# Keys' features through VectorE and DRAM, and sums over both value halves at once, in an attention and Fourier kernel

## The chip, the core and the metric

The kernel runs on one core of a Trainium2 chip. The time is in device microseconds (us) for one execution; the profile is one further execution, recorded by the hardware profiler. The core's engines are TensorE (PE in the profile; PEld are its weight loads), VectorE (DVE), ScalarE (ACT), GpSimd (POOL) and SyncE (SP), which in this kernel issues all DMAs. Each engine works off its instructions in the order in which the program has them, and waits at an instruction until its operands are ready.

## The reference

Two independent parts, written side by side into the output. The first is an attention with a memory over four segments of 512 tokens, with 32 heads of 18 features; the second is a Fourier mixing made of matrix products.

```python
q, k, v = (x @ w, split into H=32 heads of Dh=18, N=4 segments of L=512 for w in (wq, wk, wv))
phi = lambda t: jnp.where(t > 0, t + 1.0, jnp.exp(t))
g = _sigmoid(beta)
M, z = 0, 0
for s in range(N):
    qs, ks, vs = q[:, :, s], k[:, :, s], v[:, :, s]
    logits = jnp.einsum("bhqd,bhkd->bhqk", qs, ks) * scale + mask      # causal within the segment
    a_dot = jnp.einsum("bhqk,bhkd->bhqd", _softmax(logits), vs)
    pq = phi(qs)
    num = jnp.einsum("bhld,bhde->bhle", pq, M)
    den = jnp.einsum("bhld,bhd->bhl", pq, z)[..., None] + 1e-6
    outs.append(g * (num / den) + (1.0 - g) * a_dot)
    pk = phi(ks)
    M = M + jnp.einsum("bhld,bhle->bhde", pk, vs)
    z = z + jnp.einsum("bhld->bhd", pk)
a = concat(outs) @ wo
b = dft_seq_re @ (x2 @ dft_hid_re.T) - dft_seq_im @ (x2 @ dft_hid_im.T)
return jnp.concatenate([a, b], axis=-1)
```

The memory M (18x18 a head) and its normaliser z sum over all keys of the segments before. The change is about phi of the keys, the sums M and z, and the lookup num / den.

## The kernel before, in words

All products that need more than bf16 run in two or three passes: an operand is split into a high part (`hi`, rounded to fp32r) and a low part (the rest), and hi*hi, hi*lo and lo*hi are added.

The first stage projects one segment after the other, s = 0 to 3. Its order is written out by hand; every engine gets its instructions in the order of the Python code, and `later(n, ...)` puts a piece of work `n` ticks further down (there is a tick behind each projection and behind each block of values). For a segment:

- Nine projection tiles of 128 features x 512 tokens, m = 0 to 8, each a chain of 14 matmuls. Tiles 0 to 3 are queries, 4 to 7 are keys, and tile 8 holds the last 64 features of both. `open_qk` interleaves the first four; `project_qk` runs the others and evacuates all nine. The order in segments 1 to 3 is 0, 1, 2, 3, 8, 4, 5, 6, 7, and in segment 0 it is 0 to 8.
- Evacuation of a tile: ScalarE copies it to bf16 (`p`), VectorE subtracts (`r`), and later ScalarE or POOL and POOL again cut `r` into two more bf16 parts. The three go to DRAM (`qd`, `kd`) for the second stage. `p` has four buffers and `r` three.
- In segments 1 to 3 the queries also pass through phi: a Relu and an Exp on ScalarE, `scalar_tensor_tensor` on VectorE, a rounding copy to `pq_hi` on VectorE and the difference to `pq_lo` on POOL. In PSUM two engines never read one tile at a time; the program makes each wait for the other.
- In segments 0 to 2 ScalarE copies the key tiles to `kf` in fp32. They lie with features on partitions, and the sums need tokens on partitions.
- Four blocks of 128 tokens, j = 0 to 3: `project_v` (two chains of 14 matmuls over 288 columns) and its evacuation, with the two halves of `lookup` behind the two chains (segments 1 to 3). Then `k_natural` turns the block's keys with five TensorE transposes into the PSUM tile `kt`, and runs phi on the result (`kn` hi and lo). One block late, `accumulate` adds phi(k) times v into `m_ps`: three passes over five groups of 128 features, each with the eight heads that the group touches. The last block's sums run inside the next segment's `open_qk`.
- `memory` copies `m_ps` out, zeroes what lies off the heads' diagonal (POOL) and splits the result into `md_hi` and `md_lo`. `lookup` multiplies `pq` by it: three passes over five groups of 152 columns.

PSUM has eight banks: here `kt` takes two, `m_ps` two, and projections, values and lookups share four (`acc`).

The second stage, behind 235 us, is the attention within the segments, interleaved with the Fourier products; then follow the rest of these and the output product. The diff does not touch them.

Of the kernel before, what the change touches and what calls it, by code (L numbers as in the profile page):

```python
# [23 lines left out]
P = 128  # L24
# [4 lines left out]
HEAD0 = [0, 7, 14, 21, 24]  # L29
NPAIR = 108  # L30
# [8 lines left out]
def infini_attention_and_fnet(ctx: ExitStack, tc: tile.TileContext, xT, wqk, w8, wv, wo, beta, xtT, cT, hT, out):  # L39
# [10 lines left out]
    vd = [dram.tile([P, 4, 8, 220], BF16, name=f"vd{s}") for s in range(NSEG)]  # L50
    amd = [dram.tile([4, P, D], F32, name=f"amd{s}") for s in range(NSEG)]
# [15 lines left out]
    ident = const.tile([P, P], F32, name="ident")  # L67
    identity(ident)
# [74 lines left out]
    WQ = weight(wide_tile(L))  # L143
# [4 lines left out]
    for k in range(5):  # L148
        load_x(0, k)
        raw = load_w(wqk[:, :, :L], L, k)  # L150
        split_x(0, k)
        split_wk(WQ, k, raw)
    dma(g, bass.AP(tensor=beta.tensor, offset=beta.offset, ap=[[0, P], [1, H]]))
    WK, WV = weight(wide_tile(L)), weight(wide_tile(D))
    for k in range(5):
        if k < 2:
            raw = sb.tile([P, L], F32, name="r", tag="r", bufs=3)
            dma(raw, wqk[k, :, L:])
        else:
            raw = load_w(wqk[:, :, L:], L, k)  # L160
        later((1, 1, 1, 1, 2)[k], split_wk, WK, k, raw)
# [18 lines left out]

    pq_hi = sb.tile([P, 5, L], F32R, name="pq_hi")
    pq_lo = sb.tile([P, 5, L], F32R, name="pq_lo")
    zeros_r(pq_hi[64:, 4, :])
    zeros_r(pq_lo[64:, 4, :])
# [3 lines left out]
    for i in range(2):  # L188
        kn.append(tuple(sk.tile([P, D], F32R, name=f"kn{n}{i}") for n in "hl"))
        a, b = (sk.tile([P, H, 19], F32R, name=f"vn{n}{i}") for n in "hl")  # L190
        pool.memset(a.bitcast(F32)[:, :, DH:], 1.0)
        zeros_r(b[:, :, DH:])
        vn.append((a, b))
# [4 lines left out]
    md_hi, md_lo = (sb.tile([P, 5, 8, 19], F32R, name=f"md{n}") for n in "hl")  # L198
    m_ps = [ps.tile([P, 3, 8, 19], F32, name=f"m{b}", bufs=1) for b in range(2)]

    def phi(pool_, name, src, n, hi, lo):
        e = pool_.tile([P, src.shape[-1]], F32, name=f"{name}e", bufs=2)[:n]
# [3 lines left out]
        dve.tensor_copy(hi, e)  # L206
        pool.tensor_tensor(lo, e, hi.bitcast(F32), OP.subtract)
# [10 lines left out]
    FIRST, KF = {}, {}  # L218

    def warm_up():  # L220
        o = ps.tile([P, 1024], F32, name="kt", bufs=1)
# [3 lines left out]
    def open_qk(s):  # L225
        for m in range(4):
            FIRST[m] = ps.tile([P, L], F32, name="qk", tag="acc", bufs=4)
        terms = [qk_terms(s, m) for m in range(4)]
        edges = (0, 6, 14) if s else (0, 3, 6, 9, 14)
        for a, b in zip(edges, edges[1:]):  # L230
            for m in range(4):
                for n in range(a, b):
                    pe.matmul(FIRST[m], *terms[m][n], start=n == 0, stop=n == 13)  # L233
                if s and m == 0 and a:
                    accumulate(3, (2,))
# [768 lines left out]
```

## Time and profile before

| | us |
|---|---|
| median of 3 runs | 1009.86 |
| lowest, highest | 1009.55, 1011.33 |
| the profiled execution's own time | 1009.58 |
| its span in the profile | 1007.8 |

The page of the profile gives each engine's busy time and share of the span with its number of instructions, a line of the span in 40 slices, the DMA queues, and the chain of work that ended last. A group row names line, engine, operation, output <- inputs, shapes and count, then busy us and mean ns of one, then the engine's idle time ahead of it and who ended it. A timeline row is start in us, duration in us, engine, line, operation; in square brackets stands the idle time before it and its releaser. A row by windows is the stretch, its length, busy us of PE, PEld, DVE, ACT and POOL (instructions in brackets), the granted clock, the DMA share and GB/s. In a row of one line or tile the three durations are least, median and most in ns. Matmuls are pipelined, so that one's recorded duration is longer than its place in the stream; the places are read from the starts.

### The profile page before, as it was taken

How to read it: one execution, taken by the hardware profiler on the slowest of the kernel's cores; microseconds unless marked ns; L12 is line 12 of the kernel's file. 1: busy time of each engine (PE TensorE's matmuls, PEld its weight loads, DVE VectorE, ACT ScalarE, POOL GpSimd, SP SyncE). 2: the span in 40 equal slices, each digit the busy share in tenths (PEclk: the TensorE clock that was granted, in tenths of full speed). 3: DMA queues.
4: the chain of work that ended last, by engine and by line, in shares of the span. 5: the costliest groups of instructions: out<-in, count | busy, mean ns of one | idle time of the engine just before them, and what ended most of it. 6: DMA issues, size and time to landing. Idle time of an engine off the chain costs nothing.

```text
span 1007.8 us, 25664 instructions
## 1 busy us (share of the span) xinstructions
PE 997.1 (99%) x9384; PEld 931.9 (92%) x9384; DVE 735.1 (73%) x1995; ACT 710.8 (71%) x1654; POOL 641.8 (64%) x701
## 2 busy tenths in 40 slices
PE   9999999999999999999999999999999999999998
PEld 8988989899899999999999999999989999999998
DVE  6645647575678777788898778888888889998321
ACT  7656567554777778787878788886767778777243
POOL 2657585776666776766776777767767666768100
PEclk9999999999999999999999999999999999999999
DMA  7538456687467998899999998788999999987565
GB/s 254 179 101 256 183 165 236 206 277 239 128 168 198 224 220 218 195 223 241 222 260 219 239 206 185 175 211 226 226 211 235 232 245 224 257 197 183 132 160 136
DMA packets 305038, 208.92 MB, mean 207 GB/s; under 512 B 206224, under 2 KB 259600, under 8 KB 304912
## 3 DMA queue, kind: packets, MB, share of 16 engines
q1 hardware_dynamic: 304912, 207.29, 80.3%
q8 instruction: 73, 1.20, 0.5%
q14 instruction: 53, 0.43, 0.1%
HBM read 121.32 MB, written 57.93 MB: 178 GB/s over the span
## 4 chain that ended last, share of the span: by engine, by line
PE 83%; DVE 5%; ACT 5%; issue 2%; DMA 2%; POOL 2%; SPq 1%; POOLq 0%; DVEq 0%; ACTq 0%
PE d L518 38%; PE s L678 7%; PE d L80 6%; PE v L80 4%; PE pv L796 4%; PE qk L233 4%; PE d L563 3%; PE d L564 3%; PE d L565 3%; PE pv L797 2%; PE m L326 2%; PE qk L80 2%; PE look L351 1%; PE t L752 1%; PE t L755 1%
## 5 line engine op out<-in xcount | busy, mean ns | idle before, releaser
L684 DVE CUSTOM_DVE_ANT_0 s<-s,causal 128x128 f32<-128x128 f32 (+3 forms) x512 | 250.1, 499 | 80.4 <-PE s L678 73.1
L518 PE MATMUL d<-wide,chi 128*128 128x288 f32 x1408 | 266.3, 306 | 0.8 <-DVE y L587 0.8
L405 POOL TENSOR_TENSOR clo<-craw,chi 128x512 fp32r<-128x512 f32 x158 | 215.0, 1361 | 66.6 <-ACT chi L400 47.0
L518 PEld LDWEIGHTS d<-wide,chi 128*128 128x128 f32 x1408 | 211.8, 189 | 2.7 <-DVE y L587 1.0
L518 PE MATMUL d<-wide,clo 128*128 128x288 f32 x704 | 177.5, 319 | 0.0
L718 POOL TENSOR_TENSOR hl<-pf,hl 128x768 f16<-128x768 f32 x64 | 113.9, 1779 | 42.5 <-ACT hl L714 30.3
L678 PE MATMUL s<-ks,qs 108*128 108x128 bf16 (+3 forms) x512 | 134.0, 304 | 2.7 <-DVE negm L684 2.4
L764 ACT ACTIVATE phi<-t 128x384 f16<-128x384 f32 x128 | 61.7, 482 | 105.8 <-PE t L761 105.7
L707 ACT ACTIVATE pf<-s,nb 128x128 f32<-128x128 f32 (+3 forms) x256 | 128.3, 527 | 6.2
L518 PE MATMUL d<-ab,chi 128*128 128x288 f32 x640 | 126.0, 306 | 0.0
L518 PEld LDWEIGHTS d<-wide,clo 128*128 128x128 f32 x704 | 118.6, 189 | 1.7
L779 DVE TENSOR_TENSOR plo<-pf,phi 128x384 f16<-128x384 f32 (+1 forms) x128 | 115.8, 905 | 0.0
L400 ACT ACTIVATE chi<-craw 128x512 fp32r<-128x512 f32 x160 | 100.1, 626 | 6.5 <-DMA craw<-xtT 4.2
L765 ACT ACTIVATE pf<-t 128x384 f32<-128x384 f32 (+1 forms) x192 | 99.5, 518 | 5.2 <-PE t L752 5.0
L518 PEld LDWEIGHTS d<-ab,chi 128*128 128x128 f32 x640 | 98.5, 189 | 0.6
L714 ACT ACTIVATE hl<-pf 128x768 f16<-128x768 f32 (+1 forms) x128 | 87.4, 730 | 2.0
L518 PE MATMUL d<-ab,clo 128*128 128x288 f32 x320 | 84.8, 314 | 0.0
L563 PE MATMUL d<-wide,chi 128*128 128x288 f32 x256 | 84.0, 328 | 0.0
L564 PE MATMUL d<-wide,chi 128*128 128x288 f32 x256 | 75.6, 295 | 0.0
L565 PE MATMUL d<-wide,clo 128*128 128x288 f32 x256 | 75.5, 295 | 0.0
L718 DVE TENSOR_TENSOR hl<-pf,hl 128x512 f16<-128x512 f32 x64 | 70.3, 1098 | 0.0
L779 POOL TENSOR_TENSOR plo<-pf,phi 128x384 f16<-128x384 f32 x64 | 59.9, 936 | 9.3 <-ACT pf L765 8.2
(198 smaller groups left out, 2526.7 us busy)
## 6 DMA issues: line engine op xcount, KB each, us to landing
craw<-cT SPq DMA_DIRECT2D x128, 256.0 KB
ks<-kd SPq DMA_DIRECT2D x32, 432.0 KB
qs<-qd SPq DMA_DIRECT2D x32, 432.0 KB
craw<-xtT SPq DMA_DIRECT2D x32, 320.0 KB
vd<-vs SPq DMA_DIRECT2D x16, 440.0 KB
vst<-vd SPq DMA_DIRECT2D x32, 220.0 KB
qd<-p SPq DMA_DIRECT2D x16, 384.0 KB
kd<-p SPq DMA_DIRECT2D x16, 384.0 KB
```

Of the source, the lines that this page charges most:

```text
L80: pe.matmul(o, a, b, start=n == 0, stop=n == len(terms) - 1)
L400: act.activation(hi, raw[:, :4], AF.Copy)
L405: engine.tensor_tensor(lo, raw[:, :4], hi.bitcast(F32), OP.subtract)
L518: pe.matmul(o[h], a, b[:, h * 288:h * 288 + 288], start=start, stop=stop)
L563: pe.matmul(o, xh[:, k], wl[k][:, cs], start=k == 0, stop=False)
L564: pe.matmul(o, xh[:, k], wh[k][:, cs], start=False, stop=False)
L565: pe.matmul(o, xl[:, k], wh[k][:, cs], start=False, stop=False)
L678: pe.matmul(o[:, c:c + w], q[:, i * P:w], k[:, :w], start=True, stop=True)
L684: dve.tensor_tensor_reduce(o[:, c:c + w], o[:, c:c + w], CAUSAL[0][:, L - w:], scale=scale, scalar=-LOWEST, op0=OP.add, op1=OP.min, accum_ ...
L707: act.activation(f[:, FIRST_COL[i]:FIRST_COL[i] + w], o[:, c:c + w], AF.Exp, bias=nb[:, i:i + 1], scale=-1.0)
L718: engine.tensor_tensor(hl[:, 1, a:b], f[:, a:b], hl[:, 0, a:b], OP.subtract)
L779: (pool if kind == 2 else dve).tensor_tensor(lo[:, a:b], f[:, a:b], hi[:, a:b], OP.subtract)
```

## The change

- The order of the tiles is turned round: keys first (4, 5, 6, 7, 0, 1, 8, 2, 3 in segment 0; 8, 4, 5, 6, 7, 0, 1, 2, 3 in segments 1 and 2; segment 3 keeps its order). The keys' weights are loaded and split ahead of the queries'.
- phi of the keys is computed in `project_qk`, on the projected tile, as that of the queries is. VectorE transposes the result in blocks of 32x32 (`key_features`), and four DMAs a tile (two for tile 8) write the blocks to a scratch in DRAM, `kx`, in token order, in pieces of 32 features (128 bytes). Each block of 128 tokens is read back whole (`key_load`) and split into hi and lo (`key_split`). The TensorE transposes, `kf`'s copies and `kt` go.
- `accumulate` works on six groups of heads (`KEYED`), six heads or two each. The value halves hi and lo lie side by side in one tile, so that one matmul with the high keys takes both; a second takes the low keys with the high values: two passes over six groups for three over five.
- `memory` adds the two halves, zeroes off-diagonal parts, and moves the pieces by 12 small DMAs into `mg`, in the five groups of 128 features that the lookup uses. `md` holds both halves side by side.
- `lookup` takes both halves in one pass for three of the five groups; for the fifth, the low part of the queries stands in the unused partitions 64 to 127 of `pq_hi`. 11 matmuls for 15.
- PSUM: `kt` goes, `m_ps` takes three banks for two, `acc` five for four.

```diff
+KEYED = ((0, 6, 0, 0), (6, 6, 0, 6), (12, 6, 1, 0), (18, 6, 1, 6), (24, 6, 2, 0), (30, 2, 2, 6))
...
+    kx = [dram.tile([L, D], F32, name=f"kx{s}") for s in range(NSEG - 1)]
...
+    def feature_map(pool_, name, src):
+        e = pool_.tile([P, L], F32, name=f"{name}e", bufs=2)[:src.shape[0]]
         act.activation(e, src, AF.Relu, scale=-1.0)
         act.activation(e, e, AF.Exp, scale=-1.0)
         dve.scalar_tensor_tensor(e, src, 0.0, e, op0=OP.max, op1=OP.add)
-        dve.tensor_copy(hi, e)
-        pool.tensor_tensor(lo, e, hi.bitcast(F32), OP.subtract)
+        return e
+    def query_features(m, e):
+        if m < 4:
+            dve.tensor_copy(pq_hi[:, m], e)
+            pool.tensor_tensor(pq_lo[:, m], e, pq_hi[:, m].bitcast(F32), OP.subtract)
+        else:
+            dve.tensor_copy(pq_hi[:64, 4], e)
+            pool.tensor_tensor(pq_hi[64:, 4], e, pq_hi[:64, 4].bitcast(F32), OP.subtract)
+    def key_features(s, m, e):
+        t = sk.tile([P, 16, 32], F32, name="kt", tag="kf", bufs=5)
+        dve.transpose(t.rearrange("p b j -> p (b j)"), e)
+        for a in range(4) if m < 8 else (2, 3):
+            f = (m - 4) * P + 32 * a if m < 8 else L + 32 * (a - 2)
+            later(2, dma, kx[s].rearrange("(b i) f -> i b f", i=32)[:, :, f:f + 32], t[32 * a:32 * a + 32])
+    def key_load(s, j):
+        KR[j] = sk.tile([P, D], F32, name="kr", tag="kf", bufs=5)
+        dma(KR[j], kx[s][j * P:(j + 1) * P])
+    def key_split(j):
+        raw = KR.pop(j)
+        hi, lo = kn[j % 2]
+        dve.tensor_copy(hi, raw)
+        pool.tensor_tensor(lo, raw, hi.bitcast(F32), OP.subtract)
...
+    ORDER = ((4, 5, 6, 7, 0, 1, 8, 2, 3), (8, 4, 5, 6, 7, 0, 1, 2, 3), (8, 4, 5, 6, 7, 0, 1, 2, 3),
+             (0, 1, 2, 3, 8, 4, 5, 6, 7))
...
-        if s and (m < 4 or m == 8):
-            n = P if m < 4 else 64
-            c = m if m < 4 else 4
-            phi(sb, "q", o[:n], n, pq_hi[:n, c], pq_lo[:n, c])
+        keys, queries = m >= 4 and s < 3, s and (m < 4 or m == 8)
+        if keys or queries:
+            e = feature_map(*((sk, "k") if keys else (sb, "q")), o if keys or m < 4 else o[:64])
+            if queries:
+                query_features(m, e if m < 4 else e[:64])
+            if keys:
+                key_features(s, m, e)
...
-    def k_natural(j):
-        o = ps.tile([P, 1024], F32, name="kt", bufs=1)
-        js = slice(j * P, (j + 1) * P)
-        for m in range(4):
-            pe.transpose(o[:, 512 + m * P:512 + (m + 1) * P], KF[4 + m][:, js], ident)
-        pe.transpose(o[:, 384:512], KF[8][:, js], ident)
-        phi(sk, "k", o[:, 448:], P, *kn[j % 2])
...
+    def accumulate(j, which=(0, 1)):
+        (kh, kl), v = kn[j % 2], vn[j % 2]
+        for n in which:
+            for h, heads, b, at in KEYED:
+                fs = slice(DH * h, DH * (h + heads))
+                o = m_ps[b][:DH * heads, :, at:at + heads]
+                first = dict(start=b not in started, stop=True, skip_group_check=True)
+                if n == 0:
+                    pe.matmul(o, kh[:, fs], v[:, :, h:h + heads], **first)
+                else:
+                    pe.matmul(o[:, 0], kl[:, fs], v[:, 0, h:h + heads], **first)
+                started.add(b)
+    def memory():
+        t = sk.tile([6 * DH, 6, 6, 19], F32, name="mf")
+        for i, (h, heads, b, at) in enumerate(KEYED):
+            o = m_ps[b][:DH * heads, :, at:at + heads]
+            f = t[:DH * heads, i, :heads]
+            act.activation(f, o[:, 1], AF.Copy)
+            dve.tensor_tensor(f, f, o[:, 0], OP.add)
...
+                for up in (0, 64) if c == 4 else (0,):
+                    later(2, dma, mg[a - P * c + up:z - P * c + up, c, h0 - HEAD0[c]:h1 - HEAD0[c]],
+                          t[a - f0:z - f0, i, h0 - h:h1 - h])
+        def cut():
+            act.activation(md[:, :, 0], mg, AF.Copy)
+            dve.tensor_tensor(md[:, :4, 1], mg[:, :4], md[:, :4, 0].bitcast(F32), OP.subtract)
+            dve.tensor_tensor(md[:64, 4, 1], mg[:64, 4], md[:64, 4, 0].bitcast(F32), OP.subtract)
+        later(5, cut)
...
+        def two_chunks(c):
+            o = ps.tile([P, 3, 8, 19], F32, name="look", tag="acc", bufs=5)
+            kw = dict(stop=True, skip_group_check=True)
+            pe.matmul(o[:, 0:2], pq_hi[:, c, js], md[:, c], start=True, **kw)
+            pe.matmul(o[:, 0], pq_lo[:, c, js], md[:, c, 0], start=False, **kw)
+            pe.matmul(o[:, 2], pq_hi[:, c + 1, js], md[:, c + 1, 1], start=False, **kw)
+            pe.matmul(o[:, 2], pq_hi[:, c + 1, js], md[:, c + 1, 0], start=False, **kw)
+            pe.matmul(o[:, 2], pq_lo[:, c + 1, js], md[:, c + 1, 0], start=False, **kw)
+            return o
...
+        if more:
+            key_load(s, 0)
         for j in range(4):
             project_v(s, j, lookup(s, j) if s else iter(()))
             if more:
-                k_natural(j)
+                if j < 3:
+                    key_load(s, j + 1)
+                key_split(j)
             tick()
```

More of the change, by code (lines that the diff above doesn't have):

```diff
@@ L181, in infini_attention_and_fnet @@
     pq_hi = sb.tile([P, 5, L], F32R, name="pq_hi")
-    pq_lo = sb.tile([P, 5, L], F32R, name="pq_lo")
-    zeros_r(pq_hi[64:, 4, :])
-    zeros_r(pq_lo[64:, 4, :])
+    pq_lo = sb.tile([P, 4, L], F32R, name="pq_lo")
     kn = []
@@ L457, in infini_attention_and_fnet @@
             tick()
[L458 removed]
+        for n, m in enumerate(ORDER[s]):
             project_qk(s, m)
```

125 lines of the change are left out of this document (58 added, 67 removed).

## The prediction

> **What bounds the kernel now.** I read the page first, then the chain of waits over the first 240 us, then the timeline of one segment's evacuations. The change lies in the projection stage, which is the first 230 us; behind it the kernel's instructions are the same.
>
> ```profile
> span 1007.8 us, 25664 instructions
> PE 997.1 (99%) x9384; PEld 931.9 (92%) x9384; DVE 735.1 (73%) x1995; ACT 710.8 (71%) x1654; POOL 641.8 (64%) x701
> PEclk9999999999999999999999999999999999999999
> ```
>
> TensorE is busy throughout at full clock, so each matmul removed counts unless another chain takes over. The chain of waits (start, us, work) prices TensorE's pieces:
>
> ```profile
> 6.32 13.11 PE qk L233 x56
> 19.43 15.87 PE qk L80 x70
> ...
> 49.92 0.44 PE kt L284 x4
> 50.36 0.11 PE kt L285
> 50.47 1.51 PE m L326 x15
> 51.98 3.75 PE v L80 x28
> ...
> 57.79 2.32 PE qk L233 x10
> ...
> 106.86 0.63 PE look L351 x6
> ...
> 111.45 0.96 PE look L351 x9
> ...
> 117.02 5.50 PE qk L233 x24
> 122.51 1.00 PE m L326 x10
> ...
> 175.98 5.51 PE qk L233 x24
> ```
>
> A projection of 14 takes 3.17 us (15.87 / 5), five key transposes 0.55, the key sums of one block 1.51, one lookup 1.59 (0.63 + 0.96), one block of values 3.75. The segments open at 6.32, 57.79, 117.02 and 175.98: segments 1 and 2 are 59.23 and 58.96 long. The second thing to see is how one query map is evacuated (timeline, segment 2):
>
> ```profile
> 125.73 0.55 ACT L331 ACTIVATE mf<-m 128x456 f32<-128x456 f32 x1 [6.94 <-PE m L326]
> 126.54 0.59 ACT L258 ACTIVATE p<-qk 128x512 bf16<-128x512 f32 x1
> 127.16 0.69 DVE L259 TENSOR_TENSOR r<-qk,p 128x512 f32<-128x512 f32 x1 [5.03 <-ACT p L258]
> 127.89 0.60 ACT L203 ACTIVATE qe<-qk 128x512 f32<-128x512 f32 x1 [0.76 <-DVE r L259]
> 128.52 0.63 ACT L204 ACTIVATE qe<-qe 128x512 f32<-128x512 f32 x1
> 129.18 0.69 DVE L205 SCALAR_TENSOR_TENSOR qe<-qk,qe 128x512 f32<-128x512 f32 x1 [1.33 <-ACT qe L204]
> 129.91 0.43 DVE L206 CAST pq_hi<-qe 128x512 fp32r<-128x512 f32 x1
> 130.25 0.69 DVE L259 TENSOR_TENSOR r<-qk,p 128x512 f32<-128x512 f32 x1
> ...
> 144.36 1.28 POOL L207 TENSOR_TENSOR pq_lo<-qe,pq_hi 64x512 fp32r<-64x512 f32 x1 [1.36 <-DMA kd<-kd]
> ...
> 148.97 0.23 PE L351 MATMUL look<-mdl,pq_hi 128*128 128x152 f32 x1
> ```
>
> It is a ladder between two engines: r waits for p, the Relu for r, the sum in L205 for the Exp, and the next r stands behind the cast on VectorE. Nothing fills the rungs; one map takes 3.09 us (127.16 to 130.25). Today five maps a segment go through it, queries first, and the last low part (144.36 + 1.28 = 145.6) is 3.3 us ahead of the first lookup (148.97). That slack is what the change spends.
>
> **TensorE's gain.** Removed are 60 transposes: 12 x 0.55 = 6.6 us. Key sums go from 15 to 12 matmuls a block. Their 228 columns are not in the trace; between the 152-column matmul (0.101, from 1.51 / 15) and the 288-column one (0.134, from 3.75 / 28) I take 0.101, since 128 and 152 columns cost nearly the same: 12 x 3 x 0.101 = 3.6, and 1.3 at the other end. A lookup goes from 15 matmuls to 11, two of them with 304 columns (0.14): about 1.24 for 1.59, 12 x 0.35 = 4.2. Together 14.4 us.
>
> The skill would make the transposes dearer. The Trainium skill, "VectorE: DVE Perf Modes", section "The three transpose paths", gives TensorE 390 ns for a 128x128 bf16 transpose; by it 60 are worth 23 us as an estimate and the forecast below would fall by 17 us, to 1009. In this stream the fp32 one costs 0.11 us, and the row decides.
>
> **The ladder's new load.** In segments 1 and 2 all five key tiles now go through Relu, Exp, sum and a transpose before the queries come; nine maps for five. A key map is r, Relu, Exp, sum, transpose, with the transpose in the place of the cast. The trace has a smaller transpose:
>
> ```profile
> L831 DVE STREAM_TRANSPOSE ogt<-og x64: 260/286/308, 298.5 to 941.6; 128x128 f32<-128x128 f32 x64
> ...
> L769 POOL TENSOR_SCALAR_AFFINE_SELECT pf<-pf 128x512 f32<-128x512 f32 x64 | 54.0, 844 | 1.1 <-POOL hl L718 0.8
> ...
> L849 SPq DMA_DIRECT2D og<-amd x24: 568/575/584, 438.9 to 926.9; - x24
> ...
> L58 DVE TENSOR_TENSOR mdl<-mf,mdh 128x760 fp32r<-128x760 f32 x3 | 2.8, 943 | 0.0
> ...
> L358 DVE TENSOR_TENSOR nd<-nd,look 128x57 f32<-128x57 f32 x12 | 2.5, 205 | 0.1
> ...
> L332 ACT ACTIVATE mf<-m 128x152 f32<-128x152 f32 x3 | 0.9, 291 | 0.0
> ```
>
> 512 columns lie between the cast's 0.43 and 4 x 0.286 = 1.14; I take 0.70, the other fp32 operations of that size. A key map is then 3.09 - 0.43 + 0.70 = 3.36 us.
>
> Segment 1 or 2, from its opening T. The sums of the last block end at T+8.4 (before, 125.73 - 117.02 = 8.7; three matmuls fewer are 0.3). The memory is now read in six pieces: in each of three banks ScalarE copies, VectorE adds, ScalarE copies again and must wait for the add. With some 0.27 a copy (152 columns take 0.29), 0.26 an add (57 columns take 0.21) and handovers of 0.05 that is 0.9 a bank, 2.7 for today's 0.8, and the last add stands ahead of the first r: T+11.7 (today 10.1). Tile 8 takes 3.36 + 0.43, four more keys 13.4: T+28.9. The cut of the memory on VectorE follows (0.94 by today's row, 1.1 in two pieces), then four queries at 3.09: T+42.4, and the last low part on POOL 1.3 and its semaphores: T+44. TensorE itself arrives earlier: nine projections 28.6 and key sums 1.2 bring it to T+29.8, the second lookup half of the first block to T+34.8. It waits in order, in front of both lookup halves, about 9.4 us. PSUM does not stop it sooner: with five banks each projection finds its bank released. Behind the stall the first block's low key sums wait another 1 us or so, since on POOL the gate product and the value part stand ahead of the keys' low part (0 to 2 by when VectorE is done); three blocks of 3.75 + 1.24 and three sums of 1.2 end the segment at T+64.3. Against 59.23 and 58.96 that is +5.1 and +5.3.
>
> Segment 0 has five key maps and no lookup, but VectorE also splits weights there.
>
> ```profile
> 17.33:37.20 19.87, 19.87 (x96) 16.80 (x95) 15.59 (x24) 14.45 (x29) 13.27 (x11) 1.00 0.53 188
> ...
> 41.42 1.27 POOL L313 TENSOR_TENSOR vs<-vr,vs 128x576 bf16<-128x576 f32 x1 [2.31 <-ACT vs L312]
> 43.95 1.42 POOL L207 TENSOR_TENSOR knl<-ke,knh 128x576 fp32r<-128x576 f32 x1 [1.26 <-DVE knh L206]
> ...
> 45.43 0.74 PE L326 MATMUL m<-vnh,knl 128*128 128x152 f32 x5 [0.18 <-POOL knl L207]
> ```
>
> From the first r (17.33) to the end of the ninth (37.20) VectorE is busy 15.59 us. Five maps add Relu and Exp waits (1.33), sum (0.69) and transpose (0.70): 13.6, and some 1.5 of waits for ScalarE's weight pieces: the ninth r ends at 48.0. Tile 8, in seventh place, is transposed at 44; its two DMAs, the read of the scratch (on SP behind a qd write that POOL releases near 48) and the cast end near 51.5. That cast waits on VectorE with the second block's value parts behind it, but the later condition is another: the values' evacuation stands behind the ninth r, and POOL ends the first block's value part today 5.5 us after that r (42.7 for 37.2), so at 53.5, and the keys' low part at 54.9. The low sums start at 55.0 for 45.43, 9.5 later; the two later blocks are 0.85 shorter each. Segment 0 becomes 7.8 us longer, segment 3 (queries first, no key maps) 1.7 shorter.
>
> Sum: 7.8 + 5.1 + 5.3 - 1.7 = +16.5; 1009.58 (the profiled run; the median is 1009.86) + 16.6 = **1026 us**.
>
> The new order of weights (keys' loaded first), one bank more for projections and the smaller low-part tile change no instruction's time; the first 44 matmuls on the identity stay.
>
> **Queues.** SP gets 18 scratch writes, 12 memory pieces and 4 reads a segment. A write has 512 pieces as og<-amd has: 0.575 us to issue, 18 x 0.575 = 10.4; the others some 0.35. SP stands idle between its DMAs today, mostly for POOL:
>
> ```profile
> SPq L90 <- POOL p L270: 70.0, 27, 11.6
> ...
> q1 hardware_dynamic: 26938, 48.78, 62.7%
> ...
> 57.79:117.02 59.23, 58.77 (x379) 53.45 (x379) 31.53 (x70) 37.50 (x81) 38.05 (x39) 1.00 0.56 188
> ```
>
> Walked in order, SP issues the first read at T+43 and its data land before the sums at T+49, so I cost it at nothing; without that cover it is some 3 us a segment. The memory pieces (select 2 x 0.9 from the 0.844 row, 12 issues) are back by T+20; ScalarE's cut waits for them with the first query's p behind it, but comes at T+28. The p tiles wait for kd writes now queued behind four scratch writes; they land 1 to 3 us ahead of need.
>
> **Rivals.** (a) *The maps hide* and only TensorE's gain is left: 1009.6 - 14.4 = 995 us. A map would have to cost 2.6 us or less: 23 maps (5 + 9 + 9) carry 16.5, or 0.72 each. That is as if Relu did not wait for r; the timeline shows it waiting each time. A transpose of 0.43 gives back only 15 x 0.27 = 4. (b) *DMA becomes the bound.* A segment writes 18 x 512 = 9216 pieces of 128 B. Over the first 235 us a packet takes 0.627 x 16 x 235 / 26938 = 87 ns in the mean, with far larger packets; at that price they need 9216 x 0.087 / 16 = 50 us of all queues where 0.44 x 59 = 26 are free. Nearer 40 ns they just fit (23 us). At 60 ns, 35 us, segments 1 and 2 each run some 9 us over: 1026 + 18 = 1044. The Trainium skill, "DMA: Bandwidth & Descriptors", section "Specifications", says transfers below 512 B make the DMA engine read, modify and write; that speaks for (b), and no run here yet shows such writes to DRAM. (c) *Segment 0 hides its maps* behind its own values, which would make it 3.4 shorter (four blocks by 0.85) for 7.8 longer: 1015. Against it: its first values need the ninth r out of the way.
>
> **How the numbers follow.** The main case has 0.62, (b) 0.15, (c) 0.10, (a) 0.09, and 0.04 for a change lost in the noise. A comparison here tells 0.2% (2 us) from none. Transposes at 1.14 add 15 x 0.44 = 6.6, to 1033; at 0.43 take 4; wider sums add 2. With (c) below and part of (b) above: 1012 to 1040. Faster 0.09, same 0.04, slower 0.87.
>
> **What would show it.** Right: in segments 1 and 2 TensorE idles 8 to 11 us in front of the first block's lookups, released by POOL's pq_lo or VectorE's cast; the r (L289 of the changed kernel) repeats every 3.4 us over keys; the sums in L352 and L354 of block 0 wait in segment 0 for knl; phase two is as long as before. Wrong: no idle TensorE at the lookups (a); the ladder broken by waits for DMA, with the DMA share near 1 (b); r's that overlap a Relu.

## The result and the profile after

The changed kernel takes 1056.71 us (median; 1055.90 to 1059.37), the kernel before 1010.38 (1009.55 to 1011.33) in the same comparison: a ratio of 1.0463, 95% interval 1.0441 to 1.0484. It is slower by 46 us; the forecast was 16 (1026, range 1012 to 1040).

The page of the changed kernel, its span, busy times and granted clock:

```profile
span 1054.2 us, 25618 instructions
PE 1004.4 (95%) x9240; PEld 930.5 (88%) x9240; DVE 761.5 (72%) x2080; ACT 707.5 (67%) x1674; POOL 633.3 (60%) x678
PEclk9899698798999999999999999999999999999999
```

TensorE has 144 matmuls fewer, is busy 95% for 99%, and its granted clock now drops in the first quarter. Stretches by stage show where (columns as described under "Time and profile before"; the stretches are segments 0 to 3, each from its first projection matmul, and then the second stage). First before, then after:

```profile
6.08:57.63 51.55, 51.18 (x307) 45.79 (x304) 35.56 (x62) 37.20 (x74) 23.20 (x18) 1.00 0.65 212
57.63:116.85 59.22, 58.76 (x380) 53.44 (x379) 31.52 (x69) 37.33 (x81) 38.05 (x39) 1.00 0.56 188
116.85:175.82 58.97, 58.78 (x381) 53.43 (x379) 34.56 (x70) 36.80 (x81) 39.66 (x40) 1.00 0.59 194
175.82:228.50 52.68, 52.26 (x317) 46.98 (x315) 31.74 (x56) 29.91 (x64) 38.80 (x41) 1.00 0.75 244
228.50:1007.80 779.30, 771.45 (x7969) 727.65 (x7968) 600.44 (x1741) 566.99 (x1357) 499.17 (x547) 1.00 0.86 207
```

```profile
5.72:65.23 59.51, 53.80 (x275) 45.35 (x275) 40.98 (x68) 36.53 (x73) 21.24 (x18) 0.91 0.74 221
65.23:141.27 76.04, 60.70 (x333) 53.14 (x332) 40.55 (x92) 35.56 (x87) 35.74 (x32) 0.87 0.61 183
141.27:216.67 75.40, 60.72 (x333) 52.94 (x332) 42.35 (x98) 35.33 (x86) 37.63 (x33) 0.89 0.61 186
216.67:273.50 56.83, 53.84 (x299) 47.66 (x297) 36.22 (x82) 30.75 (x74) 36.82 (x32) 0.94 0.69 230
273.50:1054.20 780.70, 771.42 (x7969) 727.63 (x7968) 600.67 (x1742) 566.74 (x1356) 499.52 (x549) 1.00 0.85 207
```

The second stage is as long as before (+1.4). The segments grew by 8.0, 16.8, 16.4 and 4.2 us; the forecast had +7.8, +5.1, +5.3 and -1.7. So segment 0 came out near the computed time, and the forecast lacks 11 to 12 us in each of segments 1 and 2 and 6 in segment 3. In TensorE's timeline of segment 1 the wait at the first block's lookups is there, only longer and in pieces:

```profile
101.55 0.38 PE L394 MATMUL look<-md,pq_hi 128*128 128x304 f32 x1 [3.23 <-DVE pq_hi L213]
...
106.59 0.49 PE L396 MATMUL look<-md,pq_hi 128*128 128x152 f32 x1 [3.46 <-DVE pq_hi L213]
...
117.35 0.49 PE L396 MATMUL look<-md,pq_hi 128*128 128x152 f32 x1 [4.06 <-DVE pq_hi L213]
118.69 0.50 PE L398 MATMUL look<-md,pq_lo 128*128 128x152 f32 x1 [0.64 <-POOL pq_lo L214]
```

The last query features come 53.5 us behind the opening (118.69 - 65.23) in place of 44. VectorE's timeline of the same segment says why. Its r rows of some maps (the instructions between them are left out):

```profile
80.23 0.64 DVE L289 TENSOR_TENSOR r<-qk,p 128x512 f32<-128x512 f32 x1
83.56 0.65 DVE L289 TENSOR_TENSOR r<-qk,p 128x512 f32<-128x512 f32 x1
87.04 0.65 DVE L289 TENSOR_TENSOR r<-qk,p 128x512 f32<-128x512 f32 x1
93.44 0.69 DVE L289 TENSOR_TENSOR r<-qk,p 128x512 f32<-128x512 f32 x1 [2.99 <-ACT p L288]
...
103.36 0.69 DVE L289 TENSOR_TENSOR r<-qk,p 128x512 f32<-128x512 f32 x1 [1.96 <-ACT p L288]
...
114.00 0.69 DVE L289 TENSOR_TENSOR r<-qk,p 128x512 f32<-128x512 f32 x1 [2.60 <-ACT p L288]
```

The first maps follow each other in 3.3 to 3.5 us (forecast 3.36), then in 4.7 to 6.4, and VectorE waits for p. The waits from 60 to 275 us (who at which line, for whom: us in total, times, longest) name what p waits for:

```profile
ACT p L288 <- DMA kd<-p: 21.3, 10, 4.0
...
DVE r L289 <- ACT p L288: 19.2, 14, 3.3
```

p has four buffers, and each is free only when its kd or qd write has landed. (The kernel before has this wait too: 7.7 us, 3 times, the longest 2.7.) The writes themselves don't take longer: from the end of SP's third kd write of tile 8 to the p that waits for it are 1.56 us in segment 1 (91.18 to 92.74), and 1.56 in segment 2 of the kernel before (149.18 to 150.74). They go out later. SP's timeline in segment 2 (it opens at 141.27) shows what stands ahead of those writes:

```profile
154.28 9.98 SPq L91 DMA_DIRECT2D mg<-mf  x12
164.36 0.99 SPq L91 DMA_DIRECT2D kx<-kt  x2
165.45 0.50 SPq L91 DMA_DIRECT2D qd<-p  x1
165.99 1.87 SPq L91 DMA_DIRECT2D kd<-p  x3
...
169.24 2.16 SPq L91 DMA_DIRECT2D kx<-kt  x4
171.50 0.45 SPq L91 DMA_DIRECT2D kd<-p  x1
172.00 0.48 SPq L277 DMA_DIRECT2D qd<-qd  x1
172.52 0.61 SPq L277 DMA_DIRECT2D kd<-kd  x1
173.23 2.55 SPq L91 DMA_DIRECT2D kx<-kt  x4
175.89 0.80 SPq L91 DMA_DIRECT2D kd<-p  x1
```

The 12 memory pieces take SP from T+13 to T+23 (0.83 us each, T being the segment's opening). The DMA engines are nearly idle meanwhile (share, last column but one, 0.09), so it is SP that they occupy:

```profile
154.30:164.20 9.90, 9.90 (x45) 8.19 (x45) 6.26 (x10) 5.63 (x11) 5.75 (x8) 1.00 0.09 21
```

Behind them SP issues one tile's group after the other: four scratch writes, a kd write, two copies, later a load of x. That is 4.0 us from 169.24 to 173.23 and up to 5.5 for the later groups, with no gap of more than 0.3 us until T+52. A tile costs SP more than the 3.3 to 3.5 us that it costs the ladder.

### The profile page after: what moved, and what is told of

The parts are those of the page before. It is cut to its first block, busy times and chain, and to the rows that moved or that the text cites. A ratio compares the mean times of both kernels' runs of the same rounds, so it can differ in the third digit from the quotient of the medians.

```text
span 1054.2 us, 25618 instructions
## 1 busy us (share of the span) xinstructions
PE 1004.4 (95%) x9240; PEld 930.5 (88%) x9240; DVE 761.5 (72%) x2080; ACT 707.5 (67%) x1674; POOL 633.3 (60%) x678
## 4 chain that ended last, share of the span: by engine, by line
PE 71%; DVE 8%; DMA 5%; issue 5%; ACT 5%; POOL 3%; SPq 2%; POOLq 0%; DVEq 0%; ACTq 0%
PE d L579 36%; PE s L739 7%; PE d L81 6%; PE pv L857 4%; PE d L624 3%; PE d L625 3%; PE d L626 3%; PE pv L858 2%; PE v L81 2%; DMA kr<-kx 1%; PE t L813 1%; DMA kd<-kd 1%; SPq L91 1%; DVE r L289 1%; POOL p L303 1%
## 5 line engine op out<-in xcount | busy, mean ns | idle before, releaser
L840 POOL TENSOR_TENSOR plo<-pf,phi 128x384 f16<-128x384 f32 x64 | 59.7, 933 | 9.3 <-ACT pf L826 8.5
```

Of the source, the lines that this page charges most:

```text
L840: (pool if kind == 2 else dve).tensor_tensor(lo[:, a:b], f[:, a:b], hi[:, a:b], OP.subtract)
```

## The experiments

Three theories of the excess stand against each other. Q: SP is full of issues while the maps run, and p's buffers wait behind them. D: the DMA engines are held by the 128-byte pieces of the scratch, rival (b) of the forecast. C: the granted clock falls behind each stall and makes the rest slow. L stands for the forecast's ladder itself. All times beside these names are medians; the changed kernel's is 1056.7, and differences in brackets are from it.

**Leaving out what was added to SP** (e1, e3, e5). The scratch writes, the pieces, and both:

```diff
...
-            later(2, dma, kx[s].rearrange("(b i) f -> i b f", i=32)[:, :, f:f + 32], t[32 * a:32 * a + 32])
...
-        dma(KR[j], kx[s][j * P:(j + 1) * P])
+        dma(KR[j], wv[j])
```

```diff
-        for i, (h, heads, b, at) in enumerate(KEYED):
...
-                    later(2, dma, mg[a - P * c + up:z - P * c + up, c, h0 - HEAD0[c]:h1 - HEAD0[c]],
-                          t[a - f0:z - f0, i, h0 - h:h1 - h])
```

> Left out: the 18 scratch writes of each of segments 0 to 2; the blocks' keys are read from the value weights instead (one read of the same size a block), so the memory is summed over other numbers. Maps, transposes, splits, sums, memory pieces and lookups stay. Three theories of the 30 us beyond the forecast. Q (SP's order and issue time: memory pieces and scratch writes stand ahead of the kd and qd writes, so p's buffers come back late): the 12 us of issues a segment go, p's waits of 23 us shrink to under 8, and the time falls to 1026 to 1034. D (the DMA engines' throughput with 128-byte pieces): about the same, 1026 to 1034. C (TensorE's granted clock falls when the maps stall it, and everything behind a stall runs slower; the queue only looks busy): the ladder still stalls TensorE, the clock still falls, and the time stays above 1043.

> Left out: the 12 memory pieces of each of segments 1 to 3, so the lookups multiply by zeros; everything else stays. Q: SP's 9.7 us in front of tile 8's scratch writes go, p comes back earlier; 5 to 8 us less in each of segments 1 and 2, up to 4 in segment 3: 1036 to 1046. D: 12 small DMAs are nothing to the engines, 1053 to 1058. C: 1050 to 1058.

> Left out: both the scratch writes (the blocks' keys are read from the value weights) and the 12 memory pieces (the lookups multiply by zeros). What is left of the change is the ladder of nine maps, the merged sums and the merged lookups. The forecast costed just these, at 1026. L (the forecast's ladder was right and all its excess lies on SP): 1024 to 1031, with segments 1 and 2 at 64 to 66 us and the first lookup's end some 44 us behind the opening. M (the ladder itself was costed too low): 1034 or more. In between, 1031 to 1034, both have a share.

Measured: 1040.16 without scratch writes (-16.5), 1043.01 without pieces (-13.7), 1031.18 without both (-25.5). The time of e1 lies between C's bound and Q's range; e3 and e5 are in Q's and L's terms (e5 0.2 us past L's upper end). Segments 1 and 2 of e5, by stage:

```profile
68.00:132.36 64.36, 57.95 (x334) 51.63 (x332) 39.95 (x92) 34.68 (x87) 35.88 (x32) 0.95 0.59 194
132.36:197.30 64.94, 58.21 (x333) 51.53 (x332) 42.02 (x98) 34.68 (x87) 37.75 (x33) 0.95 0.59 194
```

They are 64.4 and 64.9 long where the forecast had 64.3 for the ladder alone, TensorE's wait for the last query features ends at T+43.5 and T+44.0 (forecast T+44), and ScalarE's wait for kd<-p is down from 21.3 us to 1.2. So the ladder was costed well, and 25 of the 30 us beyond the forecast are the added DMAs. (Segment 0 is 62.0 long in e5 and 60.9 in e3, for 59.5 in the changed kernel, though e3 leaves segment 0 as it is; that stays unexplained.) e3 also speaks against D: with all scratch writes and copies in place, and the DMA engines' share at 0.97 from 89 to 120 us, ScalarE's wait for kd<-p falls to 6.8 us. With one of the two left out the other still delays p, so the single effects, 30 together, count 5 us twice.

**What of the scratch: pieces' size, place, or number of issues** (e2, e4, e9).

```diff
-            f = (m - 4) * P + 32 * a if m < 8 else L + 32 * (a - 2)
-            later(2, dma, kx[s].rearrange("(b i) f -> i b f", i=32)[:, :, f:f + 32], t[32 * a:32 * a + 32])
+            f = (m - 4) * 4 + a if m < 8 else 16 + a - 2
+            later(2, dma, kx[s].rearrange("l f -> (l f)").rearrange("(g i x) -> g i x", i=32, x=L)[f],
+                  t[32 * a:32 * a + 32].rearrange("p b j -> p (b j)"))
```

> The scratch is written in 32 pieces of 2048 bytes a write in place of 512 of 128 bytes: the same 18 writes, bytes and waits a segment, only the order inside the scratch is another (so each block reads other features of other tokens). Q (the number of issues ahead of the kd and qd writes): an issue may fall from about 0.58 to 0.35 us, 4 us a segment, and the rest of the waits stays: 1043 to 1052. D (128-byte pieces clog the DMA engines): like the kernel without scratch writes, 1026 to 1034. C: no change, 1054 to 1058.

Measured: 1051.22 (-5.5). Sixteen times fewer pieces of the same bytes bring back a third of what leaving the writes out does; ScalarE still waits 18.8 us for kd<-p. In e2 four scratch writes take SP 1.8 to 2.0 us in segment 2, against 2.1 to 2.6, and the kd write behind them 0.4, against 0.4 to 1.3. So the small pieces cost SP some time too, but D is not the main cause.

```diff
+    WAIT = ((6, 5, 4, 4, 2, 2, 2), (7, 6, 5, 5, 4), (7, 6, 5, 5, 4))
...
-            later(2, dma, kx[s].rearrange("(b i) f -> i b f", i=32)[:, :, f:f + 32], t[32 * a:32 * a + 32])
+            later(WAIT[s][n], dma, kx[s].rearrange("(b i) f -> i b f", i=32)[:, :, f:f + 32], t[32 * a:32 * a + 32])
...
-                    later(2, dma, mg[a - P * c + up:z - P * c + up, c, h0 - HEAD0[c]:h1 - HEAD0[c]],
+                    later(4, dma, mg[a - P * c + up:z - P * c + up, c, h0 - HEAD0[c]:h1 - HEAD0[c]],
...
-        later(5, cut)
+        later(8, cut)
```

> All DMAs stay and only their place on SP changes: each tile's scratch writes come four to five projections later, behind all the keys' kd writes and right ahead of the blocks' reads, and the memory pieces come two ticks later (the cut three ticks later). Q: p no longer waits for kd behind scratch writes, the ladder runs at 3.1 to 3.4 us a map; but 18 writes now stand in front of the first read, which may cost 3 us a segment: 1028 to 1038. D: the writes load the engines just the same and closer together, 1050 to 1060. C: above 1045.

Measured: 1075.61 (+18.9). Q's number was badly wrong, in an instructive way. ScalarE's waits for kd<-p halve (10.2 us for 21.3; those for qd<-p grow from 2.1 to 5.3), but 18 scratch writes now stand between the last kd write and the first read, at 0.73 to 0.8 us each, and TensorE waits at the sums as well as at the lookups. A row of VectorE's timeline in segment 2 (opening 148.52), and two of TensorE's:

```profile
184.46 0.69 DVE L292 TENSOR_TENSOR r<-qk,p 128x512 f32<-128x512 f32 x1 [4.27 <-ACT p L291]
...
191.66 0.62 PE L397 MATMUL look<-md,pq_hi 128*128 128x304 f32 x1 [11.17 <-DVE md L386]
...
214.50 1.35 PE L355 MATMUL m<-vn,knh 128*108 128x228 f32 x6 [11.55 <-DVE knh L239]
```

The first wait ends at T+43.1, close to the forecast's T+44, but for other reasons: the cut of the memory (L386) now stands behind the eighth tile's map, and VectorE lost 4.27 us ahead of the seventh because p waited for a kd write that stood behind the moved memory pieces (SP, 171.49 to 181.05). The second wait is new. Moving issues doesn't make them cheaper; it changes what waits behind them.

```diff
-            if s and n < 8:
+            if not more and n < 8:
                 copy_parts(s - 1, 2 * n)
                 copy_parts(s - 1, 2 * n + 1)
...
+            for n in range(4 * j, 4 * j + 4) if s and more else ():
+                copy_parts(s - 1, n)
```

> The changed kernel; in segments 1 and 2 the 16 copies within qd and kd of the segment before go to SP behind the blocks of values (four a block) in place of behind the projections (two each). Nothing of the change itself moves. Q (SP is saturated with issues while the maps run, and p's buffers wait for it): 16 x 0.55 = 9 us of issues leave that stretch in each of the two segments, ScalarE's waits for kd<-p fall from 21 to under 12 us, 8 to 16 us come back: 1040 to 1048. D (the engines' work on the 128-byte pieces is the limit): 1052 to 1060.

Measured: 1041.51 (-15.2), as Q has it. ScalarE's wait in that kernel, and the DMA share (last column but one) of two stretches of 30 us in which the maps run, first in e9, then in the changed kernel:

```profile
ACT p L288 <- DMA kd<-p: 9.7, 4, 4.0
```

```profile
95.00:125.00 30.00, 22.02 (x120) 20.11 (x119) 18.55 (x45) 18.29 (x44) 16.50 (x15) 0.72 0.89 258
165.00:195.00 30.00, 21.60 (x131) 20.11 (x130) 19.87 (x49) 18.20 (x46) 17.85 (x16) 0.83 0.91 266
```

```profile
100.00:130.00 30.00, 17.40 (x88) 15.84 (x89) 14.04 (x39) 14.05 (x35) 13.32 (x11) 0.66 0.89 278
170.00:200.00 30.00, 16.34 (x74) 14.39 (x73) 13.70 (x30) 15.30 (x34) 13.70 (x12) 0.72 0.98 280
```

The copies belong to the kernel before, and moving them, with every added DMA left in place, gives back nearly as much as dropping the scratch. The copies also take their bytes along (144 KB each), and the share is near 0.9 in both kernels, so e9 by itself doesn't tell SP's issues from the engines' work. Three other readings do, for the larger part: the pieces hold SP while the engines are idle, e3 runs faster at a share of 0.97, and the kd write of tile 8 lands no later than before. So it is what SP has to issue ahead of the writes that free p. How much longer an issue takes because the engines are loaded was not separated: a kd write of a key tile (4 to 7) takes SP 0.38 to 0.53 us in segment 1 of the kernel before and 0.42 to 1.32 in the changed one. More buffers for p, or another queue for the added DMAs, were not tried.

**The clock** (e6, e17). Fillers in front of the chunks that wait; e17's:

```diff
+            def fill(n):
+                for _ in range(n if j == 0 and s < 3 else 0):
+                    pe.matmul(m_ps[2][:, 0, 8:11], ident16, ident16[:, :57], start=False, **kw)
+
+            fill(120 if c == 0 else 0)
             pe.matmul(o[:, 0:2], pq_hi[:, c, js], md[:, c], start=True, **kw)
             pe.matmul(o[:, 0], pq_lo[:, c, js], md[:, c, 0], start=False, **kw)
+            fill(120)
```

> The changed kernel with idle TensorE filled: 34 small matmuls on the identity (56 columns) ahead of the first chunk and ahead of each second chunk of the first block's lookup in segments 1 and 2, and 20 of 128 columns ahead of tile 8 in segment 0. The result is the same. C (the fall of the granted clock to 0.5 behind idle TensorE costs time on its own): the clock stays at 1.00 for most of these stretches and 6 to 16 us come back: 1040 to 1050. Not C (whoever waits on the ladder is late anyway, so the slow matmuls are hidden): 1054 to 1060, the fillers' own time included.

> The changed kernel with 120 small matmuls on the identity (57 columns, some 3.6 us by e6's 0.03 each) ahead of the first chunk and of each second chunk of the first block's lookup in segments 1 and 2, written to unused columns of a bank that is never waited for, and 40 of 128 columns ahead of tile 8 in segment 0. The result is the same. C (the lower clock is a cost of its own): the clock in the stretches 100 to 130 and 170 to 200 rises from 0.69 to 0.85 or more and the time falls by 4 to 12 us: 1044 to 1053. Not C: the clock rises and the time stays, 1054 to 1061, because TensorE waits for the maps again whatever its speed.

Measured: 1059.45 and 1060.61 (+2.7 and +3.9). e6's fillers were too short to decide: the mean clock of the stretches 100 to 130 and 170 to 200 went from 0.69 to 0.72. e17's raise it to 0.86:

```profile
100.00:130.00 30.00, 22.23 (x377) 20.62 (x374) 13.78 (x39) 13.94 (x35) 13.35 (x11) 0.89 0.88 280
170.00:200.00 30.00, 25.12 (x425) 22.75 (x424) 12.27 (x24) 14.15 (x30) 11.30 (x10) 0.83 0.92 252
```

and nothing comes back. e17 lies 8 us above C's range, so C does not hold for this kernel: TensorE meets the next late map whatever its speed. Fillers that run on when the features are there cost time of their own, so a few us of gain could be hidden under them. The Trainium skill, "TensorE: Matmul & The Clock Gate", section "HAM oscillation — how this bites in real kernels", asks for no idle gap above some 3.4 us and counts half of the throttled time as lost. The fall in the changed kernel agrees (waits of 3.2 to 4.1 us, clock 0.66 from 100 to 130), but in e5 the clock was 0.50 from 106 to 108 us behind four waits of 0.8 to 1.4 us, so one long gap is not needed. The loss is not seen here.

**The order** (e7).

```diff
-            later(2, dma, kx[s].rearrange("(b i) f -> i b f", i=32)[:, :, f:f + 32], t[32 * a:32 * a + 32])
+            later(1 if s and m == 7 else 2, dma, kx[s].rearrange("(b i) f -> i b f", i=32)[:, :, f:f + 32], t[32 * a:32 * a + 32])
...
-    ORDER = ((4, 5, 6, 7, 0, 1, 8, 2, 3), (8, 4, 5, 6, 7, 0, 1, 2, 3), (8, 4, 5, 6, 7, 0, 1, 2, 3),
+    ORDER = ((4, 5, 6, 7, 0, 1, 8, 2, 3), (0, 1, 2, 3, 8, 4, 5, 6, 7), (0, 1, 2, 3, 8, 4, 5, 6, 7),
```

> In segments 1 and 2 the tiles go 0, 1, 2, 3, 8, 4, 5, 6, 7 as in the kernel before; all else stays. L: the queries leave the ladder early, the first block's lookups no longer wait, but the last key map ends at about T+44, its scratch writes, the read and the cast follow, so the first block's sums wait for the keys at T+55 to T+58 in place of the lookups at T+35: about the same, 1048 to 1064. Order theory (keys first is what costs, since TensorE meets the lookups before the sums): 1030 to 1042.

Measured: 1062.74 (+6.0), within L's range: VectorE then waits up to 11.8 us for kr<-kx (the keys read back), and TensorE 6.3 and 7.7 us at the sums. Which of the two comes last in the ladder matters little.

**One part alone** (e8). The merged lookups in the kernel before:

```diff
-                for n, (a, m) in enumerate(((pq_hi, md_lo), (pq_hi, md_hi), (pq_lo, md_hi))):
-                    pe.matmul(o[-1][:, c - c0], a[:, c, js], m[:, c], start=c == c0 and n == 0, stop=True,
-                              skip_group_check=True)
+            pe.matmul(o[:, 0:2], pq_hi[:, c, js], md[:, c], start=True, **kw)
+            pe.matmul(o[:, 0], pq_lo[:, c, js], md[:, c, 0], start=False, **kw)
```

> The kernel before with one part of the change alone: the lookups take both memory halves per pass (12 matmuls for 15, three of them wide; the fifth group keeps its own low-part pass) and are evacuated as in the changed kernel; keys, transposes, sums and memory are those of before. By the forecast's prices 12 lookups save 12 x (15 x 0.105 - 10 x 0.105 - 2 x 0.14) = 3 us: 1006 to 1008. Rival: the third PSUM tile of a lookup, with four banks for projections, and five more small evacuations make TensorE wait: 1010 to 1016.

Measured: 1010.02, ratio 1.0008 (0.9995 to 1.0020): no change. A first half takes 0.55 us (five matmuls, 149.53 to some 150.08) where nine took 0.95, as priced, but VectorE has 11 us more to do in segments 1 to 3 (108.6 for 97.8), and TensorE now waits up to 0.8 us for it at a lookup. In these segments TensorE is busy 1.7 us less (168.1 for 169.8) and idle 1.9 more (3.0 for 1.1); why its busy time fell by 1.7 and not by 3 was not found.

**Taking both causes away** (e10 to e16). First the ladder: the next tile's p and r are issued ahead of the maps of the tile before, and the scratch writes come one tick earlier.

```diff
         dve.tensor_tensor(r, o, p0, OP.subtract)
+        if MAPS:
+            MAPS.pop(0)()
...
-            e = feature_map(*((sk, "k") if keys else (sb, "q")), o if keys or m < 4 else o[:64])
...
+            def mapped():
+                e = feature_map(*((sk, "k") if keys else (sb, "q")), o if keys or m < 4 else o[:64])
...
+            MAPS.append(mapped)
```

> The changed kernel with the maps interleaved: p and r of the next tile are issued ahead of the Relu, Exp, sum and transpose of the tile before, so that no engine waits a whole turn; a map then takes 2.4 to 2.7 us where its data are there. All DMAs stay, in nearly the same places. L (the ladder limits segments 1 and 2): they become 8 to 10 us shorter, 1032 to 1042. Q (SP does, at some 5 us a tile): they stay within 3 us, and only segment 0, where SP is not full, gains 2 to 5: 1046 to 1056.

Measured: 1055.77 (-0.9), Q's case: segment 0 is 3.1 us shorter, segments 1 and 2 are 1.7 and 4.0 longer, and ScalarE's wait for kd<-p grows to 35.6 us. So in segments 1 and 2 the ladder was not what limited the changed kernel. e11 adds e9's copies and a scratch with one contiguous write a tile and four reads a block:

```diff
+        a, at = (0, 4 * (m - 4)) if m < 8 else (64, 16)
+        later(1, dma, kx[s].rearrange("l f -> (l f)").rearrange("(p x) -> p x", x=L)[32 * at:32 * at + P - a],
+              t[a:].rearrange("p b j -> p (b j)"))
...
+        x = kx[s].rearrange("l f -> (l f)").rearrange("(g i b j) -> b i g j", i=32, b=16, j=32)
+        for b in range(4):
+            dma(KR[j][32 * b:32 * b + 32].rearrange("p (g j) -> p g j", j=32), x[4 * j + b])
```

> Interleaved maps, copies behind the blocks of values in segments 1 and 2, and the scratch in another layout: one write a tile (2048 bytes a partition, 5 issues for 18) and four reads a block (128-byte pieces, 16 for 4) that SP issues while it is otherwise idle. The result is the same. If the ladder and SP's saturation are the two causes, TensorE's gain becomes visible: segments 1 and 2 at 59 to 64 us, segment 0 at 53 to 58, in all 1010 to 1026. If the engines' time for 128-byte pieces is a cause of its own (D), the reads now wait instead: above 1032.

Measured: 1030.88, between its range and D's bound. VectorE's timeline in its segment 2 shows the interleaved map, 1.9 us, and what stops it:

```profile
144.43 0.64 DVE L291 TENSOR_TENSOR r<-qk,p 128x512 f32<-128x512 f32 x1
145.01 0.67 DVE L208 SCALAR_TENSOR_TENSOR ke<-qk,ke 128x512 f32<-128x512 f32 x1
145.71 0.71 DVE L222 STREAM_TRANSPOSE kt<-ke 128x512 f32<-128x512 f32 x1
146.34 0.65 DVE L291 TENSOR_TENSOR r<-qk,p 128x512 f32<-128x512 f32 x1
...
155.84 0.69 DVE L291 TENSOR_TENSOR r<-qk,p 128x512 f32<-128x512 f32 x1 [7.50 <-ACT p L290]
```

The fifth tile's p waits for the first kd write, and that stands behind the pieces (SP, 141.05 to 151.00). e12 leaves them out; e13 replaces them by two writes into a zeroed array in DRAM, in which each group of heads has its place on the diagonal, and three reads:

```diff
+            dma(mz[:5, :65664].rearrange("i (p x) -> p i x", x=608)[:, :, :114], t[:, :5].rearrange("p i h e -> p i (h e)"))
+            dma(mz[5, :36 * 608].rearrange("(p x) -> p x", x=608)[:, :38], t[:36, 5, :2].rearrange("p h e -> p (h e)"))
...
+            dma(mg[:, :4].rearrange("p c h e -> p c (h e)"), x[:, :, :152])
```

> e11 without the memory pieces (the lookups multiply by zeros). Maps take about 2 us each there and nothing holds p back, so all nine are done by T+32, ahead of TensorE's first lookup at T+35. If nothing else binds, segments 1 and 2 are what TensorE needs, 59.1 less 4 x (0.55 + 0.3 + 0.35) = 54.3, with some waits 55 to 58, segment 3 near 52: 1004 to 1014. If TensorE's gain was counted too high (a lookup's evacuation or the sums make new waits): 1015 to 1024.

> e11 with the memory moved through DRAM: two writes of the head blocks into a zeroed array and three reads of its five groups, 5 issues for 12. The result is the same. If the pieces' 10 us on SP are what is left in e11, p comes back 5 to 7 us earlier in segments 1 and 2 and they fall to 57 to 61, segment 3 by 2 to 4: 1012 to 1022. If the wait for the write ahead of the reads holds SP as long as the pieces did: 1027 to 1033.

> e13 with the reads of the first two blocks' keys issued one or two projections earlier, ahead of the last query writes, and the others one block earlier. The result is the same. Segment 0's sums wait 5.8 us for the first block's keys in e11: 2 to 5 us of that come back, so 1 to 5 us less than e13.

Measured: e12 1012.04, in its range; e13 1023.19, one us above its range; e14 1023.86, no gain. The pieces cost e11 19 us (1030.88 - 1012.04). In e13 segment 2 is 58.1 long, but segment 1 is 67.6, with one wait at its opening (TensorE's timeline):

```profile
74.49 1.32 PE L360 MATMUL m<-vn,knh 128*108 128x228 f32 x6 [6.84 <-DVE knh L239]
```

The last keys of segment 0 are late because the zeroing of the array, 1.4 MB, was queued ahead of their read; e14's earlier reads don't help against that. SP's issues stretch there as well: four reads of keys take it 2.64 us ahead of the zeroing (50.15) and 5.94 behind it (58.27). e15 zeroes two blocks of values later, and e16 also moves tile 8 up in segment 0:

```diff
-            if s == 0 and j == 1:
+            if s == 0 and j == 3:
```

```diff
-        later((1, 1, 1, 1, 2)[k], split_wk, WQ, k, raw)
+        later((1, 2, 2, 2, 2)[k], split_wk, WQ, k, raw)
...
-    later(4, split_w8)
+    later(1, split_w8)
...
-    ORDER = ((4, 5, 6, 7, 0, 1, 8, 2, 3), (8, 4, 5, 6, 7, 0, 1, 2, 3), (8, 4, 5, 6, 7, 0, 1, 2, 3),
+    ORDER = ((4, 5, 6, 7, 8, 0, 1, 2, 3), (8, 4, 5, 6, 7, 0, 1, 2, 3), (8, 4, 5, 6, 7, 0, 1, 2, 3),
...
+            if s == 0 and n == 6:
+                key_load(0, 0)
```

> e13 with the zeroing of the memory's DRAM array behind the last read of segment 0's keys in place of ahead of the third. The result is the same. If the 1.4 MB of zeroes held the keys' reads back, segment 1 falls from 67.6 to 58 to 61: 1013 to 1017. If not, no change: 1021 to 1024.

> e15 with tile 8 in fifth place in segment 0 (for seventh), its weights split three ticks earlier, and the first block's keys read from DRAM ahead of the last query writes. The result is the same. Segment 0's first sums wait 5.9 us for the keys in e13; 3 to 5 us of it come back: 1008 to 1013. If the earlier split of the weights delays the projections as much, as e15.

Measured: e15 1015.91, as expected; e16 1013.92, one us above its range: segment 0 became 3.4 us shorter (53.7 for 57.1), but segments 1 and 3 gave 3.9 of it back (62.1 for 59.7, 52.6 for 51.1). e16's ratio to the kernel before is 1.0037 (1.0025 to 1.0050): 43 of the 46 us are back, but no version here beats the kernel before. e15 by segments:

```profile
6.07:63.15 57.08, 51.03 (x277) 45.23 (x275) 39.59 (x68) 35.89 (x73) 21.35 (x18) 0.91 0.77 229
63.15:122.83 59.68, 56.19 (x334) 50.15 (x332) 42.63 (x92) 34.71 (x87) 36.24 (x32) 0.97 0.78 227
122.83:182.11 59.28, 56.23 (x334) 49.93 (x332) 44.86 (x98) 34.70 (x87) 38.45 (x33) 0.97 0.85 246
182.11:233.20 51.09, 50.44 (x298) 44.88 (x297) 39.29 (x83) 30.57 (x74) 37.39 (x32) 1.00 0.90 304
```

TensorE's own gain is visible in segment 3, which has no key maps: 51.09 for 52.68, -1.6 where the forecast had -1.7. In segments 1 and 2 its busy time is 2.6 us lower (56.2 for 58.8), but the segments are no shorter than before. What takes the rest there, with the clock at 0.97 and VectorE 10 to 11 us busier, was not settled.

## Why the prediction was wrong

The direction and the mechanism that it named were right; the size was not, and one step failed.

- TensorE's gain, 14.4 us. Right where it can be seen (segment 3 of e15; a lookup in e5 takes 0.54 + 0.66 us for 1.24), but never cashed in segments 0 to 2, since other waits take its place even in e15.
- The ladder's new load. Right. A key map takes 3.3 to 3.5 us (3.36), the transpose 0.70 to 0.71 (0.70); with the queues out of the way (e5) segments 1 and 2 are 64.4 and 64.9 (64.3), and the wait for the last query features ends at T+43.5 and T+44.0 (T+44). Its form was not right: TensorE waits 6.0 us in six pieces in e5's segment 1, not 9.4, and works at a lower clock between them.
- Segment 0, +7.8. Measured +8.0, and near its own way stations: the ninth r ends at 47.8 (48.0), the low sums start at 54.57 (55.0). That it is so close is partly luck. What came last was the cast of the keys (it ends at 53.0, for 51.5), 0.4 us behind POOL's value part, which the forecast had last; TensorE waited 2.2 us for tile 8's weights, which the forecast did not have; and e3, with the same segment 0, is 1.4 us longer there.
- Segment 3, -1.7. Measured +4.2; without the pieces it is 52.0 (e3) and 50.5 (e12). The pieces again.
- The queues, "so I cost it at nothing". This is the step that failed. The price of a scratch write was about right (0.55 and 0.61 us in the mean of segments 2 and 1; 0.575 taken), that of a memory piece was not (0.83; 0.35 taken, so 10 us for 4, and SP issues them until T+23 where they were to be back by T+20). The larger fault is the claim that the p tiles' kd writes "land 1 to 3 us ahead of need". In place of that, p waits 21.3 us for them, and leaving the added DMAs out (e5) gives 25.5 us back. The trace of the kernel before already has p waiting for kd in three places, so the slack was not there throughout. A walk that gives each DMA an issue time must also ask how much of SP one turn of the ladder takes: four writes, the kd write, two copies and a load are 4.0 to 5.5 us against 3.36, so each tile falls further behind, four buffers are soon used up, and the first read goes out at T+54.7 rather than T+43. e9 bears it out without touching the change: moving 16 old copies a segment gives 15.2 us back.
- Rival (b), DMA becomes the bound, had the right place and, in the main, the wrong resource. It priced the engines (87 or 60 ns a piece); 16 times larger pieces give 5.5 us back (e2), and e3 is 13.7 us faster at a share of 0.97, so that what SP issues counted for more. Its 1044 was nearer to 1057 than the main case. Rivals (a) and (c) did not happen: TensorE idles at the lookups, and segment 0 paid in full.
- The range, 1012 to 1040, took in only a part of rival (b), whose 1044 already is the main case plus 18. The measured time lies 31 above the main case.

## What to carry to other kernels

When a change adds DMAs to a queue, count its issues per turn of the loop that depends on it, the old ones included, and compare that with the turn's own length: a queue that is idle for a good part of a segment can be full just where buffers wait for it. Look for the transfers that free buffers (here kd<-p) and for waits on them in the trace before the change; put nothing in front of them that nobody waits for. Copies that are needed later belong in the idle stretch. And judge a part by what it gives once the other limit is gone: interleaving the maps was worth 0.9 us while SP was full, and up to 19 us without the pieces and with fewer issues beside the maps (e5 at 1031.2, e12 at 1012.0; e12 also moves the copies).

## What was not expected of the hardware

TensorE's granted clock fell to half not only behind waits of 3 to 4 us: in the changed kernel's segment 0 it was 0.50 from 30 to 34 us behind one of 2.2 (at 28.10), and in e5 0.50 from 106 to 108 behind four of 0.8 to 1.4. It came back after some us of unbroken work: from 118.7 in segment 1, to 1.00 from 125 to 127. It was 0.50 in the whole of this stretch of segment 1, although TensorE was busy for more than half of it:

```profile
104.00:123.00 19.00, 10.41 (x39) 9.43 (x40) 8.26 (x22) 9.26 (x22) 8.42 (x8) 0.50 0.92 281
```

Twelve small pieces between partitions of SBUF, 3 to 48 KB in the profile's issue list, took SP 0.83 us each, more than scratch writes of 64 KB in 512 pieces (0.55 to 0.61). The DMA engines' share was 0.09 meanwhile; what SP spends the time on, the profile does not show.
